# Low parts of the weights formed by TensorE, the softmax epsilon added by GpSimd, and a new order, in a windowed attention with a gated feed-forward

## The chip, the cores and the metric

One core of one Trainium2 chip runs the kernel. The metric is the device time of one execution in microseconds (us); a time "before" is the median of three runs.

## What is computed

Eight batches of eight heads, 576 positions, 64 numbers per head. Each position attends to itself and the 63 positions before it. The attention's output x (576 by 512 per batch) then goes two ways: through a causal depthwise convolution of 5 taps and a sigmoid (the gate), and through a 512 by 512 matrix (the value). Their product goes through a second 512 by 512 matrix.

```python
scores = np.where(mask, scores, -1000000000.0)
scores = scores - np.max(scores, axis=-1, keepdims=True)
attn = np.exp(scores)
attn = attn / (np.sum(attn, axis=-1, keepdims=True) + 1e-09)
x = np.matmul(attn, v)                       # then heads side by side
for k in range(K):
    gate_pre += conv_w[k][None, None, :] * xp[:, k:k + S, :]
gate = 1.0 / (1.0 + np.exp(-gate_pre))
val = x @ w_val
return (gate * val @ w_out).astype(np.float32)
```

The weights arrive as 64-bit floats, and the kernel takes their words apart itself.

## The kernel before

The attention is worked off in 16 windows w (two per batch). A window has two parts g of 5 and 4 column tiles, for each of which the kernel runs, with hh the half of the heads:

- `S(w,g)`: TensorE (PE) forms the scores, 80 or 64 small matmuls (L522), into PSUM slots `s`;
- `M(w,g),hh`: VectorE (DVE) adds the mask and takes the minimum (L543);
- `X(w,g),hh`: ScalarE (ACT) takes the exponentials and accumulates the sums of the rows (L553);
- `R(w,g)`: DVE adds 1e-9 to the sums and takes the reciprocal. The sums stand in a tile with two numbers per row, the second set to 1e-9 once; L561 reduces over the two, L562 is the reciprocal;
- `N(w,g),hh`: DVE, ACT or GpSimd (POOL) scales by it (L572, L574); `T(w,g),hh`: DVE transposes in 32x32 blocks (L580);
- `AVw_n`: PE multiplies with v, in steps of 16 matmuls (L611).

`EX` copies the result out of PSUM, `XH` rounds it to the short format float32r, and `XL` (POOL, L762) is the rest, so that a product of two numbers becomes three float32r matmuls. The convolution is `C` on DVE and ACT (L811, L814), or for two heads' pairs `K` on PE in plain float32 (L779); `SIG` is the sigmoid of a batch's gate. `V` is one block of the value matrix, 12 matmuls of 288 columns (L855); `HF` (DVE, L866) multiplies it with the gate; `HH` and `HL` split the product; `O` is one block of the output matrix, 12 matmuls of 512 columns (L921); `EO` copies it out and `DO` stores it. `LQ`, `LV` and `LW` are loads.

The weights come in eight pieces of 128 by 512, `w0` to `w3` of the value matrix and `w4` to `w7` of the output matrix (function `split_f64`). A piece takes DVE, ACT and POOL steps `h`, `k`, `b`, `c`, `p`, `u`, `l` on the words; `H` (ACT, L449) rounds the high part; `l` (L440, or L470 after `u`) gives the contribution of the low word; and the low part is then (a - high) + l, in two steps, `r` (L452, subtract) and `s` (L455, add). Of these 16 steps 12 are on POOL and four on DVE.

Nothing is scheduled by the framework: the table `ORDER` lists all steps, with the engine behind a slash, and each engine gets its instructions in that order. Each engine then runs its own list in order and waits on semaphores. PSUM has two slots `f` that `V`, `O`, `K` and fillers share. A word like `*2+11` in the table puts filler matmuls in front of the next step: here 2 big ones (512 columns, plain float32, L1034) and 11 small ones (512 columns, float32r, L1036), whose results nobody reads. Before has 10 big and 13 small fillers.

Of the kernel before, what the change touches and what calls it, by code (L numbers as in the profile page):

```python
# [8 lines left out]
F32 = mybir.dt.float32  # L9
# [18 lines left out]
    flex=dict(EO='AV', HH='AG', XH='AG', HL='G', CC='A', N='GAV', EX='AV', WR='GV', WK='GV', WL='GV', XL='G', DG='GV', C0='A', WH='VA'),  # L28
# [7 lines left out]
    half=(),  # L36
# [26 lines left out]
C2_3 S(3,1) XH3/A XL2 C3_3 X((3,0),0) K0_0 LQ10_0 C2_2 LV3 LQ11_0 CC0_1 X((3,0),1) w1r/G XL3 C3_2 M((3,1),0)
M((3,1),1) S(4,0) C2_1 w5s/G V0_0_2_0 C3_1 w1s/G C2_0 CC0_0 X((3,1),0) w6h/A C3_0 FX0 N((2,1),0)/G w7h/A R(3,0)
AV2_0 AV2_1 w6k/V V0_1_1_0 w7k/V w6b SIG0_0 T((2,1),0) N((3,0),1)/G T((2,1),1) w7b AV2_2 w6c AV2_3 AV2_4 AV2_5 w7c
AV2_6 AV2_7 AV2_8 HF0_0_2 w7p V0_0_0_0 w6p HF0_1_1 HH0_0_2_0/G M((4,0),0) HH0_1_1_0/G AV2_9 M((4,0),1) w7u AV2_10
V0_1_0_0 HL0_0_2_0 N((3,0),0)/G w6u X((3,1),1) T((3,0),1) EX4/A HL0_1_1_0 C4_4 HF0_0_0 T((3,0),0) w6l/G R(3,1)
EX5/A V0_0_1_0 C4_3 w7H HH0_0_0_0/G w7l/G HF0_1_0 C5_4 C4_2 S(4,1) N((3,1),1)/A HH0_1_0_0/A X((4,0),0) C5_3 w7r/G
V0_0_3_0 HF0_0_1 LQ12_0 M((4,1),0) N((3,1),0)/A LQ13_0 LV4 C4_1 C5_2 HH0_0_1_0/G HL0_0_0_0 w7s/G HF0_0_3 C5_1
V0_1_2_0 V0_1_3_0 HL0_0_1_0 M((4,1),1) X((4,1),0) w6H HH0_0_3_0/G C5_0 HL0_0_3_0 S(5,0) C4_0 X((4,0),1) w6r/G  # L70
T((3,1),1) T((3,1),0) AV3_0 AV3_1 AV3_2 w6s/G HF0_1_2 AV3_3 X((4,1),1) AV3_4 M((5,0),1) HF0_1_3 AV3_5 AV3_6 CB0 FX1
AV3_7 R(4,0) AV3_8 N((4,0),1)/V AV3_9 AV3_10 O128_0_0 HH0_1_2_0/A M((5,0),0) XH4/A HL0_1_0_0 HH0_1_3_0/A R(4,1)
EX6/A C6_4 EX7/A HL0_1_3_0 C6_3 T((4,0),1) S(5,1) EO128_0/A C7_4 C6_2 N((4,0),0)/G HL0_1_2_0 O256_0_0 XH5/G XH6/G
LQ14_0 X((5,0),0) M((5,1),0) T((4,0),0) C6_1 XL6 XH7/G DO128_0 N((4,1),1)/G XL4 C7_3 X((5,0),1) C7_2 O384_0_0 XL5
R(5,0) M((5,1),1) C7_1 EO256_0/A X((5,1),0) XL7 FX3 FX2 S(6,0) EO384_0/V X((5,1),1) DO256_0 T((4,1),1) C7_0 LV5
LQ15_0 O0_0_0 N((4,1),0)/G C6_0 N((5,0),1)/G M((6,0),0) T((4,1),0) SIG1_0 AV4_0 EO0_0/V M((6,0),1) AV4_1 AV4_2
AV4_3 AV4_4 AV4_5 AV4_6 AV4_7 AV4_8 R(5,1) T((5,0),1) AV4_9 AV4_10 V1_1_0_0 EX8/A N((5,1),0)/V N((5,0),0)/V DO0_0
LV6 C8_4 XH8/G EX9/A V1_0_2_0 C8_3 C9_4 XL8 XH9/G HF1_1_0 C8_2 V1_0_1_0 X((6,0),0) HF1_0_2 C9_3 HH1_0_2_0/A S(6,1)
XL9 HF1_0_1 T((5,0),0) V1_1_1_0 DO384_0 LQ16_0 HH1_0_2_1/A HH1_1_0_0/A X((6,0),1) FX4 M((6,1),0) T((5,1),0) LQ17_0
C8_1 HL1_0_2_0 HH1_0_1_0/G N((5,1),1)/G HL1_1_0_0 V1_0_3_0 HF1_1_1 X((6,1),0) R(6,0) HH1_1_1_0/G HH1_0_1_1/G  # L80
M((6,1),1) T((5,1),1) C9_2 HL1_1_1_0 V1_0_0_0 N((6,0),0)/A HL1_0_1_0 HL1_0_2_1 S(7,0) HF1_0_3 HF1_0_0 HH1_0_0_0/A
HH1_0_0_1/G X((6,1),1) N((6,0),1)/A C9_1 C8_0 HH1_0_3_0/G HL1_0_0_0 V1_1_3_0 HL1_0_1_1 HL1_0_0_1 M((7,0),1)
HL1_0_3_0 V1_1_2_0 HH1_0_3_1/G HF1_1_3 C9_0 HL1_0_3_1 R(6,1) HH1_1_3_0/A AV5_0 AV5_1 HF1_1_2 AV5_2 HL1_1_3_0 AV5_3
CB1 HH1_1_2_0/A AV5_4 N((6,1),0)/A AV5_5 AV5_6 HL1_1_2_0 AV5_7 T((6,0),0) AV5_8 AV5_9 AV5_10 N((6,1),1)/G
T((6,1),0) M((7,0),0) O896_0_0 EX10/A LV7 C10_4 XH10/G EX11/A C10_3 C11_4 XH11/G T((6,0),1) XL11 XL10 C10_2
O768_0_0 EO896_0/A C11_3 X((7,0),0) C10_1 C11_2 FX5 V2_0_0_0 C11_1 C10_0 C11_0 X((7,0),1) EO768_0/A S(7,1) DO768_0
# [24 lines left out]
M((12,1),1) T((11,0),0) LQ29_0 C18_4 HL3_1_1_0 HL3_1_3_0 M((12,1),0) HL3_1_2_0 O2048_0_0 C18_3 EO1792_0/A
# [974 lines left out]
```

## Time and profile before

| | us |
|---|---|
| median of three runs | 330.45 (328.34 to 330.98) |
| the profiled execution | 327.39 |
| its span, first to last instruction | 325.6 |
| PE busy | 311.8 |
| DVE busy | 250.3 |
| ACT busy | 245.7 |
| POOL busy | 179.5 |

The span is 1.8 us shorter than the execution's own time. Every step below is measured in the profiled execution.

### The profile page before, as it was taken

What the parts mean: (1) busy time and instruction counts of PE and PEld (TensorE: products, weight loads), DVE (VectorE), ACT (ScalarE), POOL (GpSimd) and SP (SyncE); (2) the same over time, 40 slices, a digit from 0 to 9 for tenths busy, and PEclk for the clock granted to TensorE, in tenths of its full rate; (3) what the DMA queues carried; (4) which work ended last, traced back from release to release, by engine and by line L of the source; (5) the groups of instructions that cost most, each with busy time, mean ns of one, the idle gap of its engine ahead of it and who ended that gap; (6) DMA issues with size and microseconds to landing.
All of it is one profiled execution on the core that took longest, in us unless ns stands there. A gap on an engine that the chain in (4) does not pass through costs nothing.

```text
span 325.6 us, 15010 instructions
## 1 busy us (share of the span) xinstructions
PE 311.8 (96%) x6149; PEld 263.0 (81%) x6149; DVE 250.3 (77%) x973; ACT 245.7 (75%) x835; POOL 179.5 (55%) x247
## 2 busy tenths in 40 slices
PE   7699989999999999999999899999999999999996
PEld 3355658887799877898889778898889889989985
DVE  4999989999999896999788587989786956272200
ACT  3798998999899898987899688996788663334111
POOL 4245386699858831775646815458147731761710
PEclk9799999999999999999999999999999999999999
DMA  7997765263466246652617282710243311002012
GB/s 252 321 314 197 251 190 170 71 202 88 149 203 205 69 142 194 205 181 76 195 37 229 73 251 88 206 68 31 90 137 89 142 68 48 4 32 97 2 64 97
DMA packets 28227, 45.02 MB, mean 138 GB/s; under 512 B 3968, under 2 KB 15488, under 8 KB 28160
## 3 DMA queue, kind: packets, MB, share of 16 engines
q1 hardware_dynamic: 27728, 43.60, 42.7%
q8 instruction: 48, 0.79, 1.0%
q10 hardware_dynamic: 432, 0.48, 0.5%
q14 instruction: 19, 0.16, 0.1%
HBM read 34.62 MB, written 9.44 MB: 135 GB/s over the span
## 4 chain that ended last, share of the span: by engine, by line
PE 81%; DVE 11%; ACT 4%; issue 2%; DMA 1%; ACTq 0%; DVEq 0%
PE f L921 32%; PE f L855 29%; PE av L611 10%; PE s L522 8%; DVE p L543 3%; DVE gp L811 3%; ACT p L553 2%; DMA st<-in_w_val_dram 1%; PE f L1034 1%; PE f L1036 1%; DVE pts L580 1%; DVE hf L866 1%; DVE w0l L440 0%; ACT xh L239 0%; ACT x L239 0%
## 5 line engine op out<-in xcount | busy, mean ns | idle before, releaser
L553 ACT ACTIVATE p<-p,nm 128x96 f32<-128x96 f32 x288 | 103.9, 364 | 4.7 <-DVE nm L543 4.5
L811 DVE SCALAR_TENSOR_TENSOR gp<-av,cw,gp 128x575 f32<-128x575 f32 (+3 forms) x120 | 93.4, 801 | 6.8 <-ACT gp L814 5.9
L855 PE MATMUL f<-xl,wv_hi 128*128 128x288 f32 x256 | 77.9, 304 | 0.6 <-DVE hf L866 0.5
L855 PE MATMUL f<-xh,wv_hi 128*128 128x288 f32 x256 | 75.5, 295 | 0.7 <-issue 0.7
L855 PE MATMUL f<-xh,wv_lo 128*128 128x288 f32 x256 | 75.4, 294 | 0.0
L884 POOL TENSOR_TENSOR h_lo<-hf,h_hi 128x288 fp32r<-128x288 f32 (+2 forms) x80 | 54.3, 693 | 19.8 <-ACT h_hi L239 19.2
L543 DVE CUSTOM_DVE_ANT_0 p<-s,mask 128x96 f32<-128x96 f32 x288 | 54.6, 250 | 6.8 <-PE s L522 6.4
L921 PE MATMUL f<-wo_hi,h_lo 128*128 128x512 f32 (+1 forms) x148 | 59.3, 400 | 0.0
L762 POOL TENSOR_TENSOR xl<-x,xh 128x576 fp32r<-128x576 f32 x32 | 45.6, 1435 | 24.0 <-ACT xh L239 23.5
L921 PE MATMUL f<-wo_lo,h_hi 128*128 128x512 f32 (+1 forms) x148 | 57.8, 390 | 1.0 <-issue 1.0
L921 PE MATMUL f<-wo_hi,h_hi 128*128 128x512 f32 (+1 forms) x148 | 57.7, 390 | 0.0
L553 ACT ACTIVATION_READ_ACCUMULATOR p<-p,nm 128x1 f32 x288 | 54.3, 189 | 0.0
L855 PEld LDWEIGHTS f<-xl,wv_hi 128*128 128x128 f32 x256 | 48.0, 188 | 3.6 <-DVE hf L866 1.0
L866 DVE TENSOR_TENSOR hf<-f,gp 128x288 f32<-128x288 f32 x64 | 28.5, 450 | 28.3 <-PE f L855 20.7
L855 PEld LDWEIGHTS f<-xh,wv_lo 128*128 128x128 f32 x256 | 48.1, 188 | 0.9 <-issue 0.8
L855 PEld LDWEIGHTS f<-xh,wv_hi 128*128 128x128 f32 x256 | 48.1, 188 | 0.5
L574 POOL TENSOR_TENSOR p<-p,rc 128x384 f32<-128x384 f32 (+1 forms) x38 | 35.0, 927 | 23.6 <-DVE rc L562 19.9
L522 PE MATMUL s<-ktb,qtb 64*32 64x96 f32 x2304 | 37.2, 248 | 5.5 <-DVE nm L543 3.2
L611 PEld LDWEIGHTS av<-pts,v 32*64 32x64 f32 x2560 | 35.1, 130 | 8.3 <-issue 5.3
L580 DVE STREAM_TRANSPOSE pts<-p 128x480 f32<-128x480 f32 (+1 forms) x64 | 38.2, 610 | 4.1 <-PE av L611 3.0
L522 PEld LDWEIGHTS s<-ktb,qtb 64*32 64x32 f32 x2304 | 29.5, 105 | 13.8 <-issue 12.7
L611 PE MATMUL av<-pts,v 32*64 32x96 f32 (+2 forms) x2560 | 39.2, 244 | 0.1
(129 smaller groups left out, 411.1 us busy)
## 6 DMA issues: line engine op xcount, KB each, us to landing
out_dram<-ot SPq DMA_DIRECT2D x35, 256.0 KB, 3.1
qtb<-in_qT_dram SPq DMA_DIRECT2D x30, 288.0 KB, 3.8
ktb<-in_kT_dram SPq DMA_DIRECT2D x30, 288.0 KB, 4.0
v<-in_vw_dram SPq DMA_DIRECT2D x64, 96.0 KB, 3.2
v<-in_vw_dram SPq DMA_DIRECT2D x64, 80.0 KB, 3.1
st<-in_w_val_dram SPq DMA_DIRECT2D x4, 512.0 KB
st<-in_w_out_dram SPq DMA_DIRECT2D x2, 1024.0 KB, 6.5
out_dram<-ot SPq DMA_DIRECT2D x2, 128.0 KB
```

The costliest lines, as they stand in the source:

```text
L522: nc.tensor.matmul(sp_t[m, hh][z * Q:z * Q + Q, t, :], lhsT=held("qt", i)[r, c:c + Q], rhs=held("kt", i)[r, c:c + KW], start=True, stop=True)
L543: nc.vector.tensor_tensor_reduce(out=pe[:, t, :], in0=sp_t[u][:, t, :], in1=mask_of(w, n0 + t), scale=-SCALE, scalar=3.0e38, op0=ALU.add, ...
L553: nc.scalar.activation(out=pe[:, t, :], in_=pe[:, t, :], func=AF.Exp, scale=-1.0, bias=nm[:, t:t + 1], accum_out=su[:, t:t + 1])
L574: MUL[e](out=pe, in0=pe, in1=rc.unsqueeze(2).broadcast_to([P, ng, KW]))
L580: nc.vector.transpose(out=pts_t[w, hh][:, n0 * KW:n1 * KW], in_=p_t.pop(u).rearrange("p t k -> p (t k)"))
L611: nc.tensor.matmul(av_t[w, z // 2][hh * D:(hh + 1) * D, c + lo * Q:c + hi * Q], lhsT=v_t[w][z * Q:z * Q + Q, hh, m % 2, m // 2 - KEYS[th][ ...
L762: SUB[e](out=batch_tile(xl_t, "xl", b, F32R)[:, hp, :], in0=x_t[i // 2][:, i % 2, :], in1=xh_t[b][:, hp, :].bitcast(F32))
L811: nc.vector.scalar_tensor_tensor(out=acc, in0=av(i, 0, S - back), scalar=col, in1=acc, op0=ALU.mult, op1=ALU.add)
L855: nc.tensor.matmul(vp_t[u][:, 0:NH], lhsT=w[:, c, js], rhs=x[:, c, hs], start=(a + z == 0), stop=(a + z == NM - 1))
L866: nc.vector.tensor_mul(out=hf, in0=free_f[-1][:, 0:NH], in1=gp_t[b][:, jb, hs])
L884: SUB[e](out=h_lo[:, jb, dst:dst + hi - lo], in0=hf_t[u][:, lo:hi], in1=h_hi[:, jb, dst:dst + hi - lo].bitcast(F32))
L921: nc.tensor.matmul(op_t[key][:, 0:cs.stop - cs.start], lhsT=h[:, jb, col:col + P], rhs=w[:, jb, cs], start=(a + z == 0), stop=(a + z == NM ...
```

## The change

The low part of every weight piece is formed on PE: three matmuls into a slot `f` add identity times a (plain float32), minus identity times the high part, and identity times `l` (both float32r). This is the step `e`; the step `s` is now a copy of the result out of PSUM, on ACT (five) or DVE (three). Steps `r` are gone. Two more constant matrices, `plus` and `minus`, are made on ACT. The tile of the sums has one number per row; a new step `Z` adds 1e-9 to it, on POOL (22 times) or DVE (10), and `R` is the reciprocal alone. The table `ORDER` is written anew, with 7 big and 42 small fillers, and was planned with the loads of instruction pieces placed by where PE's sequencer stands; the code that did that is not part of the kernel. The buffers of the convolution's diagonal matrices are named otherwise, with the same two in use.

```diff
-    sums = [const.tile([P, 2, PARTS[1], 2], F32, name=f"sums{n}") for n in range(4)]
-    for t in sums:
-        nc.vector.memset(t, 1.0e-9)
+    sums = [const.tile([P, 2, PARTS[1]], F32, name=f"sums{n}") for n in range(4)]
     ident = const.tile([P, P], F32, name="ident")
     make_identity(nc, ident)
+    plus = const.tile([P, P], F32R, name="plus")
+    minus = const.tile([P, P], F32R, name="minus")
+    nc.scalar.copy(out=plus, in_=ident)
+    nc.scalar.activation(out=minus, in_=ident, func=AF.Copy, scale=-1.0)
...
+    ON_PE = ('w0', 'w1', 'w2', 'w3', 'w4', 'w5', 'w6', 'w7')
...
+        if on_pe:
+            def rest(_):
+                g = low_t[name] = free_f.pop(0)
+                nc.tensor.matmul(like(g), lhsT=ident, rhs=like(t["af"]), start=True, stop=False)
+                nc.tensor.matmul(like(g), lhsT=minus, rhs=hi, start=False, stop=False)
+                nc.tensor.matmul(like(g), lhsT=plus, rhs=like(t["lr"]), start=False, stop=True)
+
+            def out(e):
+                free_f.append(low_t.pop(name))
+                COPY[e](out=lo, in_=like(free_f[-1]))
+            r1 = op(name + "e", ("P", 1319), rest, [hi_, lw], take=[("ps_f", name)], prio=prio)
+            return [hi_, op(name + "s", pick("EO", A=95 + 427 * c, V=70 + 535 * c), out, [r1],
+                            free=[(tag, name), ("ps_f", name)], prio=prio)]
...
+        def e_z(e):
+            BOTH[e].tensor_scalar(out=sums_of(m), in0=sums_of(m), scalar1=1.0e-9, scalar2=None, op0=ALU.add)
+        z2 = op(f"Z{m}", pick("Z", G=100, V=150), e_z, xs, prio=prio, port="VG")
+
         def e_r(_):
             rc = rc_t[m] = sb("rc", [P, 2, ng], f"rc{w}_{g}", bufs=4)
-            nc.vector.tensor_reduce(out=rc, in_=sums_of(m), axis=mybir.AxisListType.X, op=ALU.add)
-            nc.vector.reciprocal(out=rc, in_=rc)
-        r2 = op(f"R{m}", ("V", 318), e_r, xs, prio=prio)
+            nc.vector.reciprocal(out=rc, in_=sums_of(m))
+        r2 = op(f"R{m}", ("V", 165), e_r, [z2], prio=prio)
```

Of the table, the start, before and after:

```diff
-LC LW1_0 LQ0_0 LQ1_0 LQ0_1 LW0_0 w2h/A LQ1_1 cwh/V cwk/V w2k/V w2b cwb w2b LW1_1 cwc w2c LQ2_0 w2p w2H w2l/V cwH *3+1
...
+LC LW1_0 LQ0_0 LQ1_0 LW1_1 LQ1_1 LQ0_1 LQ2_0 LW0_0 LQ3_0 cwh/V w2h/V w2k/V w2b cwk/G w2c w2p w2l/V w2H w3h/A w3k/G
+*2+11 S(0,0) cwb M((0,0),0) M((0,0),1) *0+4 w2e *0+2 S(0,1) w2s/V cwc w3b cwp w3c w3p M((0,1),0) M((0,1),1) w3l/V
```

The first place is PE's list between the first two score blocks. In the kernel before, the last matmuls of S(0,0) (tiles s_0_0 and s_0_1) are followed at once by those of S(0,1) (s_1_0 and s_1_1):

```order
L522 MATMUL s_0_0_178<-ktb_84,qtb_80 32x96
L522 MATMUL s_0_1_179<-ktb_84,qtb_80 32x96
L522 MATMUL s_1_0_260<-ktb_83,qtb_79 32x96
L522 MATMUL s_1_1_261<-ktb_83,qtb_79 32x96
L522 MATMUL s_1_0_260<-ktb_83,qtb_79 32x96
```

In the changed kernel the same place holds fillers (L1064) and the three matmuls of piece w2's low part (L488 to L490, into f):

```order
L544 MATMUL s_0_0_191<-ktb_84,qtb_80 32x96
L544 MATMUL s_0_1_192<-ktb_84,qtb_80 32x96
L1064 MATMUL f_64<-h_lo 128x512 x4
L488 MATMUL f_64<-w2a,ident 128x512
L489 MATMUL f_64<-wv_hi,minus 128x512
L490 MATMUL f_64<-w2l,plus 128x512
L1064 MATMUL f_65<-h_lo 128x512 x2
L544 MATMUL s_1_0_257<-ktb_83,qtb_79 32x96
L544 MATMUL s_1_1_258<-ktb_83,qtb_79 32x96
```

Six fillers and a low part now stand ahead of S(0,1) on PE; five more low parts stand in the same way before the first V block, and two (w7, w6) between V blocks of the first batch.

The second place is the start of ACT's list, before:

```order
L951 DMA cwords<-in_conv_w_dram 128x40
L336 DMA qtb_80<-in_qT_dram 128x448
L337 DMA ktb_84<-in_kT_dram 128x448
L414 ACT_TABLE_LOAD
L414 ACTIVATE w2m<-st_141 128x512
```

and in the changed kernel:

```order
L979 DMA cwords<-in_conv_w_dram 128x40
L341 DMA qtb_80<-in_qT_dram 128x448
L260 ACT_TABLE_LOAD
L260 CAST plus<-ident 128x128
L261 ACTIVATE minus<-ident 128x128
L342 DMA ktb_84<-in_kT_dram 128x448
L458 CAST wv_hi<-w2a 128x4x128
```

The load of a k tile that S(0,0) needs now stands behind the table load and the two new constants on ACT.

## Rows read from the trace of the kernel before

**Rows 1.** The page: busy us (share of the span) by engine.
```profile
PE 311.8 (96%) x6149; PEld 263.0 (81%) x6149; DVE 250.3 (77%) x973; ACT 245.7 (75%) x835; POOL 179.5 (55%) x247
```

**Rows 2.** The ending chain in order of time: start us, us, what.
```profile
69.13 0.38 DVE hf L866
...
69.55 1.85 PE f L855 x12
...
72.59 2.43 PE av L611 x119
...
322.64 0.37 ACT ot L239
```

**Rows 3.** PE by stretches: from:to, length, PE busy (instructions), clock, DMA, GB/s.
```profile
0.00:12.90 12.90, 8.14 (x152) 1.00 0.87 304
12.90:16.40 3.50, 3.50 (x5) 0.51 0.96 214
16.40:72.50 56.10, 52.00 (x1295) 1.00 0.65 201
72.50:322.60 250.10, 248.12 (x4704) 1.00 0.37 115
```

**Rows 4.** The same chain: one block or several of AV, S, V, O.
```profile
97.09 4.97 PE f L855 x36
102.06 1.13 PE s L522 x68
...
116.14 0.93 PE s L522 x56
117.07 2.19 PE av L611 x112
...
252.98 8.43 PE f L921 x36
...
269.41 9.57 PE f L855 x72
```

**Rows 5.** PE's timeline: first fillers, S(0,0), fillers at 12.8 us, one K block.
```profile
1.45 5.15 PE L1034 MATMUL f<-ident 128*128 128x512 f32 x6 [1.45 <-POOL ident masks.py:199]
...
7.52 1.25 PE L522 MATMUL s<-ktb,qtb 64*32 64x96 f32 x80 [0.68 <-DMA ktb<-in_kT_dram]
...
12.79 3.65 PE L1034 MATMUL f<-ident 128*128 128x512 f32 x4
15.45 1.49 PE L1036 MATMUL f<-h_lo 128*128 128x512 f32 x2
...
36.10 2.69 PE L779 MATMUL f<-x,dg 128*128 128x288 f32 x10
```

**Rows 6.** The same chain: fillers between steps of AV0.
```profile
23.40 1.06 PE f L1034 x2
24.45 0.23 PE f L1036
```

**Rows 7.** ACT's timeline at the start (ACTq: its DMA issues).
```profile
1.74 0.45 ACTq L337 DMA_DIRECT2D ktb<-in_kT_dram  x1
2.22 1.28 ACT L414 ACT_TABLE_LOAD   x1 [2.22 <-issue]
```

**Rows 8.** Groups by line: busy us, mean ns, idle before.
```profile
L561 DVE TENSOR_REDUCE rc<-sums 128x10 f32<-128x20 f32 x16 | 2.6, 163 | 1.2 <-ACT p L553 1.1
L455 DVE TENSOR_TENSOR wv_lo<-w0m,w0l 128x512 fp32r<-128x512 f32 x1 | 0.7, 679 | 0.0
L452 POOL TENSOR_TENSOR w0m<-w0a,wv_hi 128x512 f32<-128x512 f32 x1 | 1.3, 1278 | 0.0
L455 POOL TENSOR_TENSOR cl<-cwm,cwl 128x20 fp32r<-128x20 f32 x1 | 0.2, 223 | 0.0
```

**Rows 9.** PE's timeline: the two longest waits after 72.5 us.
```profile
122.28 0.50 PE L921 MATMUL f<-wo_lo,h_hi 128*128 128x512 f32 x1 [0.96 <-issue]
180.26 0.29 PE L855 MATMUL f<-xh,wv_hi 128*128 128x288 f32 x1 [0.74 <-issue]
```

More of the change, by code (lines that the diff above doesn't have):

```diff
@@ L150 @@
+EO4352_0/A O4480_1_0 DO4352_0 CB7 FX15 EO4480_1/A DO4480_1 CB6 FX14
 """.split()
@@ L400, in tile_window_attention_gated_ffn @@
     lows = []
+    ON_PE = ('w0', 'w1', 'w2', 'w3', 'w4', 'w5', 'w6', 'w7')
+    low_t = {}
     def split_f64(name, words, rows, n, hi, lo, tag, load, prio, free=()):
+        on_pe = name in ON_PE
         t = {}
@@ L412, in head @@
                 t[x + "f"] = t[x].bitcast(F32)
+            t["lr"] = t["l"].bitcast(F32R) if on_pe else t["lf"]
             if e == "A":
@@ L439, in low @@
             if e == "V":
-                stt(out=t["lf"], in0=u, scalar=2.0 ** -52, in1=t["mf"], op0=ALU.mult, op1=ALU.mult)
+                stt(out=t["lr"], in0=u, scalar=2.0 ** -52, in1=t["mf"], op0=ALU.mult, op1=ALU.mult)
             else:
-                nc.gpsimd.tensor_scalar(out=t["lf"], in0=u, scalar1=2.0 ** -52, scalar2=None, op0=ALU.mult)
-                nc.gpsimd.tensor_mul(out=t["lf"], in0=t["lf"], in1=t["mf"])
+                nc.gpsimd.tensor_scalar(out=t["lr"], in0=u, scalar1=2.0 ** -52, scalar2=None, op0=ALU.mult)
+                nc.gpsimd.tensor_mul(out=t["lr"], in0=t["lf"], in1=t["mf"])
         def like(x):
@@ L465, in number @@
             def number(_):
-                nc.scalar.activation(out=t["lf"], in_=t["low"].bitcast(mybir.dt.uint32), func=AF.Copy, scale=2.0 ** -52)
+                nc.scalar.activation(out=t["lr"], in_=t["low"].bitcast(mybir.dt.uint32), func=AF.Copy, scale=2.0 ** -52)
             lw = [pw, op(name + "u", ("A", 110 + 470 * c), number, [a], prio=prio)]
             def low(e):
-                MUL[e](out=t["lf"], in0=t["lf"], in1=t["mf"])
+                MUL[e](out=t["lr"], in0=t["lf"], in1=t["mf"])
             at = pick("WR", G=130 + 1065 * c, V=70 + 535 * c)
@@ L549, in e_x @@
             def e_x(_, u=u, hh=hh):
[L550 removed]
+                su = sums_of(m)[:, hh, :]
                 pe, nm = p_t[u], nm_t.pop(u)
@@ L696, in e_cv @@
                     lo = back if y == 0 else 0
-                    nc.tensor.matmul(g[:, lo:NH], lhsT=dg[:, (KP.index(hp) * TAPS + kk) * P:(KP.index(hp) * TAPS + kk + 1) * P],
+                    nc.tensor.matmul(g[:, lo:NH], lhsT=dg[:, (hp % 2 * TAPS + kk) * P:(hp % 2 * TAPS + kk + 1) * P],
                                      rhs=x(t0 + lo - back, t0 + NH - back), start=back == 0, stop=kk == 0)
@@ L778, in e_cv @@
                         lo = back if half == 0 else 0
-                        nc.tensor.matmul(g[:, lo:NH], lhsT=dg[:, (KP.index(hp) * TAPS + kk) * P:(KP.index(hp) * TAPS + kk + 1) * P],
+                        nc.tensor.matmul(g[:, lo:NH], lhsT=dg[:, (hp % 2 * TAPS + kk) * P:(hp % 2 * TAPS + kk + 1) * P],
                                          rhs=x_t[i // 2][:, i % 2, half * NH + lo - back:half * NH + NH - back],
@@ L782, in attention @@
                 cv = op(f"K{i}_{half}", ("P", 500 * (TAPS - end)), e_cv, [ex, dgo[hp], xl_o if half else None], take=[("ps_f", (i, half))], words=4 * (TAPS - end) + 1,
-                        prio=cp)
+                        free=[(f"dg{hp % 2}", hp)] if half else [], prio=cp)
+                if half:
+                    cv.deps.append(last_cv)
+                last_cv = cv
                 def e_cc(e, half=half):
@@ L969, in tile_window_attention_gated_ffn @@
     KP = sorted({i % NHP for i, c in enumerate(CFG["conv"]) if c == "K"})
-    dg = const.tile([P, max(len(KP), 1) * TAPS * P], F32, name="dg")
+    dg = const.tile([P, 2 * TAPS * P], F32, name="dg")
     dgo = []
@@ L978, in e_dg @@
             t = slice(hp * TAPS, (hp + 1) * TAPS)
-            MUL[e](out=dg.rearrange("p (t n) -> p t n", n=P)[:, KP.index(hp) * TAPS:(KP.index(hp) + 1) * TAPS, :], in0=ident.unsqueeze(1).broadcast_to([P, TAPS, P]),
+            MUL[e](out=dg.rearrange("p (t n) -> p t n", n=P)[:, hp % 2 * TAPS:(hp % 2 + 1) * TAPS, :], in0=ident.unsqueeze(1).broadcast_to([P, TAPS, P]),
                    in1=cw[:, t].unsqueeze(2).broadcast_to([P, TAPS, P]))
-        dgo.append(op(f"DG{hp}", pick("DG", V=740, G=1450), e_dg, [cwo], prio=CFG["dg"][hp], port="VG"))
+        dgo.append(op(f"DG{hp}", pick("DG", V=740, G=1450), e_dg, [cwo], take=[(f"dg{hp % 2}", hp)], prio=CFG["dg"][hp], port="VG"))
     w_ops = [[], []]
```

203 lines of the change are left out of this document (101 added, 102 removed).

## The prediction

> **What bounds the kernel now.** I read the page first, then the chain that ended last in order of time, then PE's busy time by stretches. On the page PE is busy for 96% of the span, DVE for 77%, ACT for 75% [rows 1]; 96% is a mean, so the next question is where the rest lies. The chain in order of time says where: up to 69.55 us it keeps going through DVE (the last such piece is an hf), and from there to 322.64 it is PE alone, until the last copy out [rows 2]. So the kernel has two halves with different rules. From 72.59 on (PE begins AV3, the products of window 3) the end is "when AV3 starts, plus the PE work behind it". In that stretch PE idles 250.10 - 248.12 = 1.98 us. Ahead of it PE idles 4.76 + 4.10 = 8.86 us, and for 3.5 us it ran at half its clock (0.51: the 1.2 GHz level) [rows 3]. What other engines save counts only ahead of AV3, and only as far as PE is not itself late there.
>
> I therefore make the sum in two terms: the time at which PE reaches AV3, and what is lost behind it.
>
> **PE's work behind AV3** is the same in both tables: 21 S blocks, 13 AV, 56 V, 37 O (two of half width), no low part; one small filler is new (0.23 [rows 6]). Changes from a block of small matmuls (S, AV) to V, O or a filler cost about 0.18 each: 36 V matmuls behind an S take 4.97, by the rate of 72 of them (9.57/72 = 0.133 each) 4.79 [rows 4]. There are 30 such changes behind AV3 in either table. So this part differs by 0.2 us, plus waits.
>
> **PE's work ahead of AV3.** Block times at full clock: S 1.13 or 0.93, AV 2.19, V 12 x 0.133 = 1.60, O matmul 8.43/36 = 0.234 [rows 4], K 2.69 less its overlap of some 0.02, 2.67 [rows 5]. A big filler: the first three took 5.15, 1.72 each; two more with two small ones, nearly all at the half clock, took 15.45 + 1.49 - 12.79 = 4.15 [rows 5]; so 1.72 is a price at the low level and 0.86 one at the high level. Alone behind an AV step it took 1.06 [rows 6], which is 0.86 and the change of 0.2. A small filler is 0.23 there; I take 0.215 in a run of them. A low part has no row. It has one plain float32 matmul of 512 columns, like a big filler, and two float32r ones, like two O matmuls: 0.86 + 0.47 = 1.33. Its bounds are 1.42, by K's 2.67/5 = 0.53 for 288 columns scaled to 512 (0.95), and 1.53 by the lone filler above; below, 0.70, three O matmuls. I take 1.33, since the big filler has the same shape and type.
>
> After, ahead of AV3: 11 S (6 x 1.13 + 5 x 0.93 = 11.4), AV0 to AV2 (6.6), 4 K (10.7), 8 V (12.8), 8 low parts (10.6), 7 big fillers (6.0), 41 small ones (8.8), 13 changes from small matmuls at 0.2 (2.6), the start at 1.45, and the low level at first: 2 big ones at 1.72 and some 3 small ones at twice their time (2.4). Sum 73.3.
>
> Before, by the same prices: S, AV, K, V as above (41.5), 10 big (8.6), 13 small (2.8), 18 changes (3.6), the start 1.45, three big ones at the low level (2.6), and half of the 3.4 us at half clock (1.7): 62.3. With the 8.86 us of idle time that is 71.1; the trace has 72.6. The sum is 1.5 short, by small steps between fillers and AV steps, of which there are fewer after.
>
> So after, **PE is full from the start to AV3 even if it never waits**, and reaches it at 73.3 where before it was at 72.6 with 8.9 us of waiting. Low parts and fillers fill the gaps, and a little more. Next, one wait that the change adds. ACT now issues the load of a k tile behind its table load (1.28) and two small casts (some 0.3 each, worked out from the 0.2 of small operations [rows 8]), so at some 3.6 instead of 1.74 [rows 7]. S(0,0) waited for just this kind of load before, 0.68 until 7.52 [rows 5]. The fillers ahead of it end at 1.45 + 3.4 + 3 x 0.43 + 8 x 0.215 = 7.9. With the load 1.9 later S(0,0) would start at up to 9.4, and if the queue of transfers is the limit rather than the issue, at 7.9. I take 8.8, 0.9 of waiting; behind S(0,0) stand all of PE's fillers and low parts, so it passes on to AV3 whole. AV3 at 74.2: **+1.6 us**, between 0 (the low part at 0.70, the load hidden: 73.3 - 5.0 would be less than DVE allows, below) and +6 (gaps stay, below).
>
> **What the other engines save.** DVE loses 32 reduces of about 0.16 (5.0) and four adds or subtracts of 0.68; it gains three copies of about 0.7 and ten additions of some 0.16 to 0.2, and takes over a few copies and scalings from ACT. POOL loses 12 steps of 1.28 (15.4) and gains 22 small additions of about 0.22, the size of its 128x20 operation [rows 8]. Ahead of the first sigmoid, which the V blocks wait for through hf, this makes DVE's list shorter by seven reduces (1.1) and two full operations (1.4), less three additions (0.5): about 2 us. Before, DVE was the pace there, so DVE alone would allow AV3 at 70.6. PE doesn't: its sum is 73.3. That is why I cost the whole relief at nothing: the cover that hides it is PE's new work, and if that were gone, it would be worth those 2 us. Z adds a hop X to POOL to DVE to the chain of each part; behind AV3 its cover is that DVE and ACT have 250 and 246 us of work for 325 [rows 1].
>
> **Waits behind AV3.** Of the 1.98 us, 0.96 and 0.74 stand as "issue": in mid block, with nothing to wait for [rows 9]. The first comes two us behind S and AV back to back, 56 and 112 recorded matmuls in 3.1 us, each with its weight load [rows 4], the second by the table behind S(12,0) and the first steps of AV9; that looks like instructions that arrive late. The new table has seven such neighbours of S and AV behind AV3, the old six, so the risk is still there, and the table was planned to keep clear of it. Between all gone (-2.0) and one more of the larger size (+1.0) I take -0.5.
>
> The Trainium skill, "Runtime: NRT & Kernel Launch", section "Instruction fetch mechanics", says that instructions stream in by blocks of 256 and that this is hidden, because the sequencer issues more slowly than the blocks arrive. This case's trace speaks against it where small matmuls stand thick: 0.96 and 0.74 us without another cause [rows 9]. If the rule held, the two waits would be something else, the new table could do nothing about them, and this term would be 0, not -0.5.
>
> **Sum.** +1.6 + 0.2 - 0.5 = +1.3 on the profiled execution's 327.39: 328.7. The median of the runs shown is 330.45, 0.9% above the profiled one; for the time to be measured I put the same 1.3 us on the median: 331.7, rounded to 331.5.
>
> **The rivals.** About 1% (3.3 us) is what a measurement of this kernel can tell from no change; faster and slower mean by more than that.
>
> First rival, slower: low parts wait in PE's queue. Each waits for its high part from ACT and its product l from DVE or POOL, and everything behind it on PE waits too: the next S, hence M, X and all that follow. For it speaks that PE's list is full, so that a gap can't be made up; before, gaps of 8.86 us stood in the same stretch [rows 3]. Against it: between S blocks PE has slack against DVE (DVE's list is as long as PE's there), and fillers stand where waits were planned. If half of the old gaps stay, AV3 comes 4.4 later: 331.7 + 4.4 = 336. It decides from gaps of 2.0 us on (1.3 + 2.0 = 3.3). Chance 0.25, with a half-clock spell of 3.5 us at the start, as before, as a smaller form of it (1.7).
>
> Second rival, faster: PE's work ahead of AV3 is overpriced, DVE stays the pace and gives its 2 us, and the waits behind AV3 go: -2.0 - 2.0 = -4.0, 326.5. For it: DVE in the chain up to 69.5 [rows 2]. Against it: the low part would have to cost 1.33 - 2.7/8 = 1.0 or less, under what its float32 matmul and two O matmuls took; and there is no more than 1.98 us to gain behind AV3. Chance 0.10.
>
> Third rival, the table's care for instruction pieces does nothing, or the seven dense spots stall more: then 332 to 333, inside my own case.
>
> **How the numbers follow.** My case, within 1% of before, has 0.65; slower 0.25; faster 0.10. The range goes from 328.0 (the waits gone, the low part cheap: -2.5) to 336.0 (half the gaps stay), which leaves out some 0.1 on each side.
>
> **What would show it right or wrong.** Right: PE's first AV3 matmul at 73 to 76 us; PE idle ahead of it under 3 us in place of 8.9; a low part with 1.3 to 1.5 us; 250 us from AV3 to the last matmul. Wrong: AV3 before 72 us (then DVE set the pace and PE was overpriced), AV3 after 77 us with waits in front of low parts or of S(0,0), a half-clock spell after 8 us, or more than 3 us of "issue" behind AV3. POOL's additions would be wrong at nothing if R or N are seen waiting for them with PE idle behind.

## The result and the profile after

The changed kernel took 332.56 us (median of 20 runs, 329.72 to 334.48), the kernel before, beside it on the same chip, 330.49 (20 runs, 326.12 to 334.59). Between the medians that is 2.07 us, 0.63%; the ratio is 1.0104, with an interval of 1.0074 to 1.0134. Ratios and intervals, here and below, leave out the executions that lie more than 1.5% above the fastest of the same kernel (of the kernel before 7 of the 20), while medians are those of all. So it is slower by about 1%, at the edge of what can be told from no change, and inside the range of the prediction, 1.1 us above its number. The profiled executions lie further apart: 327.39 before (span 325.6) and 331.37 after (span 329.6). The 4.0 us between them are what can be followed in rows; the medians say that about half of that is typical.

The page after, for [rows 1], with one row of its queues (packets, MB, share):

```profile
PE 321.3 (97%) x6204; PEld 272.0 (83%) x6204; DVE 252.6 (77%) x949; ACT 237.8 (72%) x818; POOL 183.8 (56%) x272
...
q8 instruction: 49, 0.80, 1.0%
```

PE has 9.5 us more to do. The second row is used further down: 49 pieces of instructions, 0.80 MB, so 16 KB each. PE by stretches, for [rows 3] (from:to, length, PE busy with its instructions, clock, DMA share, GB/s), cut at the start of AV3 and once more where the half-clock spell lay before:

```profile
0.00:12.90 12.90, 11.47 (x169) 1.00 0.89 296
12.90:16.40 3.50, 3.50 (x23) 1.00 0.78 256
16.40:78.00 61.60, 58.84 (x1332) 1.00 0.64 188
78.00:326.60 248.60, 247.46 (x4702) 1.00 0.36 114
```

Two things changed places. Ahead of AV3 PE does 11.47 + 3.50 + 58.84 = 73.81 us of work where it did 63.64, its idle time falls from 8.86 to 1.43 + 2.76 = 4.19, the half-clock spell is gone, and AV3 comes at 78.0 instead of 72.6: 5.4 later. Behind it the last copy out begins 248.6 us later instead of 250.1: 1.5 less, and PE idles 1.14 instead of 1.98. 5.4 - 1.5 = 3.9, but for rounding the 4.0 between the profiles.

The ending chain in order of time, for [rows 2, 4, 6] (start us, us, what):

```profile
8.07 1.12 PE s L544 x69
...
10.32 0.86 PE f L488 x2
11.18 0.23 PE f L489
11.41 0.23 PE f L490
...
28.83 1.46 PE s L544 x68
...
51.00 7.06 DMA ktb<-in_kT_dram
58.06 0.14 issue
58.20 1.12 PE s L544 x63
...
64.33 8.14 PE f L883 x60
72.47 0.86 PE f L488 x2
...
78.02 2.19 PE av L636 x116
...
326.63 0.37 ACT ot L242
```

A low part takes 0.86 + 0.23 + 0.23 = 1.32, as priced (the trace has four matmuls for it, since the plain float32 one shows as two). Up to 58 us the chain passes through loads, the last of them that of a k tile, and no longer through DVE: the load that S(4,0) needs began to be issued at 51.00. PE's waits say what that cost (engine, line, what for: us in total, times, longest):

```profile
PE s L544 <- DMA ktb<-in_kT_dram: 1.7, 1, 1.7
PE f L1062 <- POOL ident masks.py:199: 1.4, 1, 1.4
PE f L1064 <- POOL h_lo L912: 1.0, 1, 1.0
PE av L636 <- DMA v<-in_vw_dram: 0.6, 1, 0.6
PE av L636 <- DVE pts L605: 0.3, 1, 0.3
```

There is no "issue" among them, which is time in which the engine waited for nothing that the profile shows; before, PE had three such waits, 3.1 us together, two of them in [rows 9]. The 1.0 is new: a small filler behind S(12,0) at 178.8 us, which reads h_lo and stands until POOL has written it. The 1.7 is S(4,0); SP's timeline shows why its load is late:

```profile
37.30 12.52 SPq L362 DMA_DIRECT2D v<-in_vw_dram  x16
49.86 0.58 SPq L393 DMA_DIRECT2D st<-in_w_out_dram  x1
...
51.00 0.44 SPq L342 DMA_DIRECT2D ktb<-in_kT_dram  x1
```

LV2 and LV3 are 16 transfers, 0.78 us apart on average in SP's queue, and LW3 and LQ9 stand behind them. S(4,0) is begun at 56.11, and waits until 58.20.

### The profile page after: what moved, and what is told of

It reads as the page before. It is cut to its first block, busy times and chain, and to the rows that moved or that the text cites. A ratio compares the mean times of both kernels' runs of the same rounds, so it can differ in the third digit from the quotient of the medians.

```text
span 329.6 us, 15091 instructions
## 1 busy us (share of the span) xinstructions
PE 321.3 (97%) x6204; PEld 272.0 (83%) x6204; DVE 252.6 (77%) x949; ACT 237.8 (72%) x818; POOL 183.8 (56%) x272
## 4 chain that ended last, share of the span: by engine, by line
PE 88%; DMA 6%; SPq 2%; POOL 2%; DVE 1%; issue 1%; ACT 0%; ACTq 0%; POOLq 0%
PE f L949 31%; PE f L883 31%; PE av L636 11%; PE s L544 9%; DMA st<-in_w_out_dram 3%; PE f L1064 2%; DMA ktb<-in_kT_dram 2%; PE f L804 2%; SPq L362 2%; PE f L488 1%; PE f L1062 1%; DMA v<-in_vw_dram 1%; POOL h_lo L912 1%; DVE p L565 0%; POOL h_hi L249 0%
## 5 line engine op out<-in xcount | busy, mean ns | idle before, releaser
L599 POOL TENSOR_TENSOR p<-p,rc 128x480 f32<-128x480 f32 (+1 forms) x38 | 34.7, 921 | 15.6 <-DVE rc L587 15.1
L636 PE MATMUL av<-pts,v 32*64 32x96 f32 (+2 forms) x2560 | 38.3, 244 | 1.0 <-DMA v<-in_vw_dram 0.6
```

Source lines behind the costliest of these rows:

```text
L599: MUL[e](out=pe, in0=pe, in1=rc.unsqueeze(2).broadcast_to([P, ng, KW]))
L636: nc.tensor.matmul(av_t[w, z // 2][hh * D:(hh + 1) * D, c + lo * Q:c + hi * Q], lhsT=v_t[w][z * Q:z * Q + Q, hh, m % 2, m // 2 - KEYS[th][ ...
```

## The experiments

Two theories on the 5.4 us at AV3. **P:** PE's own list sets AV3, so what is taken off PE ahead of it comes off its start. **Q:** a chain of loads, ACT and DVE sets it, and PE only fills up. And one question on the table: are the "issue" waits a matter of where instructions stand, and what would they cost. The kernel before ran beside each group; its medians were 329.63 (e1 to e4), 330.40 (e5 to e8) and 330.17 (e9 to e12). An AV3 time is that of its first matmul. From a single profile it is good to about 1 or 2 us: AV2, ahead of which the changed kernel, e1 and e9 have the same lists, begins at 59.25, 57.65 and 56.92, and executions of the changed kernel alone have spans from 327.9 to 332.7.

**e1: the low parts of w6 and w7 back on POOL.** They are the two between V blocks just ahead of AV3, 2.64 us of PE.

```diff
-    ON_PE = ('w0', 'w1', 'w2', 'w3', 'w4', 'w5', 'w6', 'w7')
+    ON_PE = ('w0', 'w1', 'w2', 'w3', 'w4', 'w5')
-... w7e ... w7s/A ... w6e ... w6s/V
+... w7r/G ... w7s/G ... w6r/G ... w6s/G
```

> The changed kernel, but the low parts of w6 and w7 alone are formed by POOL in two steps, as in the kernel before. My theory (PE is full from about 59 us on, so what it is spared there comes off the end): PE's list loses 2 x 1.32 us; AV3 starts 2.6 us earlier than 78.0, the time falls by 2 to 3 us (0.6 to 0.9%). Rival (the low parts lie in gaps that other engines leave): no change beyond 0.5 us, or slower, because POOL has 5 us more to do while it also splits the products of the first batch.

334.47 us, 1.0164 (1.0107 to 1.0222). AV3 began at 73.70, 4.2 us earlier than in the changed kernel. Its 160 matmuls in PE's timeline (start us, us, what, and in brackets the idle time before with what ended it):

```profile
73.70 0.38 PE L636 MATMUL av<-pts,v 32*64 32x96 f32 x8
74.38 0.81 PE L636 MATMUL av<-pts,v 32*64 32x96 f32 x40 [0.29 <-DVE gp L839]
76.34 1.21 PE L636 MATMUL av<-pts,v 32*64 32x96 f32 x72 [1.16 <-DVE pts L605]
77.96 1.29 PE L636 MATMUL av<-pts,v 32*64 32x64 f32 x40 [0.42 <-issue]
```

Of the 4.2, AV2 had 1.6 already. From the first matmul of AV2 to that of AV3 PE took 16.05 us instead of 18.70, shorter by 2.65 where 2.64 were taken off: up to there PE's list is full, and P holds. But AV3 itself then stood, mostly for DVE, and its last matmul came at 78.96 instead of 79.99, so counted from AV2 0.6 later. What PE was spared had become waits. From 77.60 to 84.60 PE then ran at half its clock:

```profile
77.60:84.60 7.00, 6.64 (x114) 0.51 0.27 73
84.60:329.00 244.40, 242.34 (x4469) 1.00 0.36 114
```

7.0 us at the 1.2 GHz level do the work of 3.5, so the gaps in AV3 cost more than their length in this execution. They are not the whole loss: two of the six executions had a mean clock of 1.000, with spans of 330.3 and 333.9. e4 and e9, with the same edit, came out alike (below): all three are 0.6% over the changed kernel's 1.0104, so by the times these two low parts are better on PE, as the rival had it.

**e2: the k tile of S(4,0) ahead of the v tiles in SP's queue.**

```diff
-CC0_0 K0_1 LQ8_0 LV2 LV3 LW3 LQ9_0 X((3,0),1)
+CC0_0 K0_1 LQ8_0 LQ9_0 LV2 LV3 LW3 X((3,0),1)
```

> The changed kernel with one load moved: the q and k tiles LQ9, which S(4,0) needs, go ahead of the v loads LV2 and LV3 and of the w_out words LW3 in SP's list. My theory (16 v transfers occupied SP's queue from 37.3 to 49.9 us, so LQ9 was issued at 50.5 and S(4,0) stood at 56.1 until 58.2): the wait of 2.1 us in S(4,0) goes, AV3 starts at about 76, the time falls by 1.5 to 2 us, if v arrives in time for AV2. Rival (PE would next wait for something else there, the hf of the first V block behind the sigmoid): the wait moves to V0_0_1 or AV2 and the time falls by less than 0.7 us.

332.92 us, 1.0110 (1.0058 to 1.0163). In PE's waits the one for the k tile shrank, and a longer one took its place:

```profile
PE av L636 <- DVE gp L839: 2.7, 1, 2.7
...
PE s L544 <- DMA ktb<-in_kT_dram: 0.7, 1, 0.7
```

LW3, now last in SP's queue, had its words in late (issued at 50.59, 6.32 us), DVE's step on w6 waited for them, and so did what stands behind it on DVE, which AV waited for. AV3 came at 79.05. That is the rival's outcome: the wait moved to AV2. Of the loads near 50 us, the one that went last was waited for in both orders.

**e3: no filler behind S(12,0).**

```diff
-HL3_0_0_1 *0+1 V3_0_3_0
+HL3_0_0_1 V3_0_3_0
```

> The changed kernel without the one small filler that stands behind S(12,0). It reads h_lo, which POOL writes just then, and PE idled 1.0 us in front of it at 177.8. My theory: the wait and the filler go (1.0 + 0.2 to 0.5), the time falls by 1.0 to 1.5 us. Rival (the V block behind it would wait for the same: its slot f is freed by hf): PE idles there all the same and nothing changes.

332.27 us, 1.0039 (0.9984 to 1.0093). The 1.0 us wait for h_lo is gone and nothing came in its place there: from the first matmul of S(12,0) to that of the next V block PE took 1.13 us instead of 2.58. A gain in the whole time is not shown. By the medians this run lies 0.8% above the kernel before, the changed kernel 0.63%; from AV3 to the last copy out its profile has 248.4 us, the changed kernel's 248.6; and e10, with the same edit, came out at 1.0069.

**e4: e1, e2 and e3 together.**

> The three edits of e1 to e3 together. My theory (each takes its time off the same full engine, one after the other): they add up, -5 to -6 us against the changed kernel, 1% faster than the kernel before or a little less. Rival (what PE is spared is lost again to DVE's pace ahead of AV3): no more than -3 us.

335.64 us, 1.0171 (1.0109 to 1.0232), the rival's outcome. AV3 began at 75.18, and its last matmul came at 79.74. The three waits are gone or shorter, and others stand there: 1.6 for pts, 1.5 for gp, and 0.8 for wo_lo, which POOL now makes late.

**e5: ACT's and DVE's first steps on w4 moved behind work that is ready.** Ahead of AV0 ACT stood 2.5 us for w4's words, whose transfer took 8.87.

```diff
-w0c w4h/A X((1,0),0) X((1,0),1) w0H w4u
+w0c X((1,0),0) X((1,0),1) w0H w4h/A w4u
...
-w0p w4k/V N((0,1),1)/V
+w0p N((0,1),1)/V
...
-w0l/V Z(1,0)/G
+w0l/V w4k/V Z(1,0)/G
```

> The changed kernel with ACT's first step on piece w4 (w4h, which waits for the words of w_out) behind the exponentials X(1,0) and w0H, and DVE's w4k behind w0l. In the changed kernel ACT stood 2.5 us in front of w4h until the words had landed at 22.7 us. New theory Q (the start is paced by a chain through loads, ACT and DVE, and PE's new work lies mostly in its gaps): that wait goes, AV3 starts 1 to 2.5 us earlier than 78.0, the time falls by 1 to 2 us. My first theory P (PE's own list ahead of AV3 is full and sets AV3's start): no change of AV3's start beyond 0.5 us.

332.28 us, 1.0066 (1.0035 to 1.0098), AV3 at 77.61, 0.4 earlier: no more than P expected, and not the 1 to 2.5 of Q. The waits ahead of AV3 were now 1.1 for ACT's gp in front of low parts and 0.7 of "issue": another exchange.

**e6: the new table with no low part on PE.** All eight go to DVE and POOL, on the engines of the kernel before.

```diff
-    ON_PE = ('w0', 'w1', 'w2', 'w3', 'w4', 'w5', 'w6', 'w7')
+    ON_PE = ()
```

> The new table, but no low part on PE: every e and s is again a subtraction and an addition on the engines of the kernel before (12 on POOL, 4 on DVE), at the places where e and s stood; fillers as in the changed kernel. Theory P: PE's list loses 8 x 1.32 = 10.6 us ahead of AV3, so AV3 starts some 4 us earlier (until the next limit) and the time falls by 3 to 4 us. Theory Q: PE only idles more (its idle time ahead of AV3 rises from 4.2 to about 13 us), AV3's start stays within 1.5 us of 78.0 or comes later, for POOL and DVE get 18 us back, and the time is the same or up to 2 us longer.

351.34 us, 1.0650 (1.0586 to 1.0714), which neither theory had. AV3 began at 85.60, 7.6 later, and its last matmul came at 90.15; ahead of it PE idled 14.0 us, about as Q had it. PE's waits:

```profile
PE av L636 <- issue: 5.9, 6, 1.7
PE av L636 <- DVE pts L605: 4.2, 2, 2.6
PE s L544 <- DVE nm L565: 3.9, 3, 2.7
```

POOL was busy for 201.1 us instead of 183.8, and with ACT it makes up the chain from 62 to 95 us. In this table the low parts on PE are thus worth far more than their price. And the "issue" waits came back, with 32 matmuls fewer ahead of the same S and AV blocks.

**e7: the new table without fillers.**

```diff
-... *2+11 S(0,0) ... *0+4 w2e *0+2 S(0,1) ...
+... S(0,0) ... w2e S(0,1) ...
```

> The changed kernel without any filler matmul (7 big, 42 small, together 16 us of PE with those at the low clock level). Theory P: PE reaches AV3 earlier by what fillers pushed back, 3 to 6 us, less what half-clock spells cost (1.7 us for each 3.4 us). Theory Q: AV3's start moves by less than 1.5 us; PE's idle time ahead of it rises by over 8 us, and the granted clock shows at least one half spell more, so the time is the same or 1 to 3 us longer.

356.26 us, 1.0766 (1.0684 to 1.0848), far longer than either theory had it; of Q the idle time and the half-clock spells came true. AV3 came at 84.7, with 17.5 us of idle time ahead of it, and the stretch behind it, whose only edit is one filler, took 17.8 us longer. PE by stretches:

```profile
0.00:84.60 84.60, 67.09 (x1448) 0.86 0.62 193
84.60:351.00 266.40, 253.28 (x4701) 0.98 0.33 106
...
104.00:105.40 1.40, 1.40 (x97) 1.00 0.92 281
105.40:109.00 3.60, 0.03 (x1) 0.77 0.24 91
109.00:114.20 5.20, 5.19 (x51) 0.50 0.23 64
```

(The last three rows are another cut, around one wait.) Of the 17.8, 13.12 - 1.14 = 12.0 are idle time and 253.28 - 247.46 = 5.8 work at half clock. "issue" is the largest of its waits, 19.3 us in 12 places over the whole span:

```profile
PE av L636 <- issue: 12.0, 7, 3.6
PE s L544 <- DMA ktb<-in_kT_dram: 7.9, 3, 7.4
PE s L544 <- issue: 6.0, 4, 2.2
...
PE f L949 <- issue: 1.3, 1, 1.3
```

The longest, in the middle of an AV step, from 105.43 to 109.01:

```profile
109.01 1.30 PE L636 MATMUL av<-pts,v 32*64 32x96 f32 x42 [3.58 <-issue]
```

The transfers by queue, of 106.5 to 107.0 us (queue: packets, MB, share), and the stretch ahead of them, in the form of the stretches:

```profile
q8 instruction: 1, 0.02, 11.7%
...
105.40:106.30 0.90, 0.03 (x1) 1.00 0.85 328
```

PE had been dry for over 1.0 us when this piece began to move, and went on 2.0 to 2.5 us after that, at half clock. Along the whole spans of five kernels (before, after, e6, e7, e12) PE has 33 "issue" waits of 0.25 us or more (3, 0, 6, 12, 12). In all 33 a piece began to move 1.7 to 3.6 us before the wait ended, counted from the start of its half microsecond, nearly always 2.4 to 3.2. A kernel has 48 or 49 pieces in some 330 us, one in 7 us, so that is no chance meeting: "issue" here is the wait for instructions.

The single records of the five traces settle it. Count PE's matmuls, weight loads and semaphore instructions from 0: in 32 of the 33 waits the first instruction that was late has the same place in a run of 256, number 193. So a piece holds 256 instructions, and these waits stand where one piece ends. All 32 ended 1.3 to 1.6 us after the last byte of the piece had landed, and at the boundaries without a wait PE never went on sooner than 1.25 us after it. (The 33rd, 2.23 us at 15.24 in e7, has neither mark and is something else.) In the median a piece began to move 1.1 us after PE had begun on the one ahead of it, and moved for about 1 us; with the 1.4 behind the landing that makes some 3.5 us. A run of 256 that PE works off faster mostly ends in a wait: of the 21 runs that held PE for less than 2.2 us, 18 did, and of the 182 of over 4 us, 5. Those 21 are S and AV blocks and little else. In the changed kernel the shortest run holds PE for 3.39 us, and there is no wait.

Where PE needed longer for the 256 and waited all the same, the piece had mostly started late, and there the transfer engines were mostly full. In the 2 us ahead of the 32 pieces their busy share is 0.58 on average, ahead of the others 0.41, but in 7 of the 32 it is under 0.1. Other transfers seem to add to these waits, then, and are not needed for one.

**e8: the sums as before, without Z.**

```diff
-    sums = [const.tile([P, 2, PARTS[1]], F32, name=f"sums{n}") for n in range(4)]
+    sums = [const.tile([P, 2, PARTS[1], 2], F32, name=f"sums{n}") for n in range(4)]
+    for t in sums:
+        nc.vector.memset(t, 1.0e-9)
...
-            nc.vector.reciprocal(out=rc, in_=sums_of(m))
+            nc.vector.tensor_reduce(out=rc, in_=sums_of(m), axis=mybir.AxisListType.X, op=ALU.add)
+            nc.vector.reciprocal(out=rc, in_=rc)
```

> The changed kernel with the sums as before: two numbers a row, DVE reduces and takes the reciprocal, no step Z on POOL or DVE. Prediction on record (the relief of DVE is worth nothing): within 0.7 us. Rival 1 (DVE paces the start, its 5 us less count): 1 to 2 us longer than the changed kernel. Rival 2 (the hop over POOL costs, since DVE waited 1.2 us for Z and POOL's additions stood 7.4 us for ACT's sums): 0.5 to 1.5 us shorter.

332.53 us, 1.0088 (1.0045 to 1.0131), AV3 at 77.7: the same, as predicted. Z is worth nothing either way, though DVE waits for it (3.4 us in two places in the changed kernel).

**e9: e1 with six small fillers where each of the two low parts stood.**

```diff
-... w7r/G S(5,0) ... w6r/G AV3_0
+... w7r/G *0+6 S(5,0) ... w6r/G *0+6 AV3_0
```

> The run e1 (low parts of w6 and w7 on POOL) with six small fillers (1.3 us) on PE at each of the two places where these low parts stood. In e1 PE waited 1.2 us for DVE's pts ahead of AV3, its granted clock then stood at the half level from 77.7 to 84.5 us, and AV3 came no earlier. Theory Q (DVE and POOL set AV3's start, and PE's low parts also keep its clock up): with fillers the half-clock spell is gone and the time falls by 1 to 3 us against e1, to that of the changed kernel within 1 us. Rival (POOL's added work is what e1 lost): no change against e1, 334 to 335 us.

334.28 us, 1.0166 (1.0113 to 1.0218). AV3 came at 75.76, and its last matmul at 77.81, 2.2 us earlier than in the changed kernel; all of it is there at AV2 already (56.92 for 59.25), and the twelve fillers make the way from AV2 to AV3 as long as the low parts did (18.84 us for 18.70). But POOL, with the two pieces back, is late with wo_lo (PE's timeline, then PE by stretches):

```profile
82.10 0.50 PE L949 MATMUL f<-wo_lo,h_hi 128*128 128x512 f32 x1 [1.78 <-POOL wo_lo L464]
```

```profile
75.70:83.20 7.50, 5.72 (x235) 1.00 0.27 70
83.20:86.70 3.50, 3.50 (x10) 0.51 0.43 139
```

1.8 of waiting and 1.7 of half clock take the gain back, so the time is that of e1, as the rival had it. In this execution, then, what the low parts of w6 and w7 on PE buy is not AV3 but wo_lo in time for the first O block; e4 waits for wo_lo too (0.8), e1 does not.

**e10: e3 and e5 together. e11: e10, with the loads of k tiles and weight words ahead of v tiles in two places.**

```diff
-LV1 LW0_1 S(2,0)
+LW0_1 LV1 S(2,0)
...
-LQ8_0 LV2 LV3 LW3 LQ9_0
+LQ8_0 LQ9_0 LW3 LV2 LV3
```

> The changed kernel with the edits of e3 (the late filler gone) and e5 (w4h later). If each keeps its gain (e3 0.6%, e5 0.4% by their medians against the changed kernel's 1.0104), they add up to about 1.0000 of the kernel before; if both gains were the spread between executions, 1.005 to 1.010.

> e10 with SP's list mended at two places: LQ9 and the words LW3 both ahead of the v loads LV2 and LV3 (16 transfers, 12.5 us of SP's queue), and the words LW0_1 ahead of LV1. In e2 LQ9 alone went ahead, LW3 fell behind, and DVE then waited for its words (w6) until 57.5 us, so that PE waited 2.7 us for DVE ahead of AV2. Theory Q (the start is paced by loads through DVE): neither wait is left, AV2 starts 1.5 to 2.5 us earlier than 59.3, the time falls by 1.5 us or more against e10. Rival P (PE's own list): less than 0.7 us, as in e2.

e10: 332.14 us, 1.0069 (1.0025 to 1.0113), AV3 at 78.85: by what was put on record, the gains of e3 and e5 were the spread between executions. e11: 333.77 us, 1.0126 (1.0056 to 1.0196), though its profiled execution has the shortest span of all changed versions, 328.6. In it AV2 begins at 56.23, 3.0 earlier than in the changed kernel, but AV3 only 0.8 earlier, at 77.25. In both the "issue" waits are back (1.5 and 2.4 us). No version beat the kernel before.

**e12: the low parts of w0 to w5 on PE in the table of before.** Sums, w6 and w7 as before; each `r` becomes an `e`, and four `s` go to ACT or DVE.

```diff
-S(0,0) w2r/V ... w2s/G
+S(0,0) w2e ... w2s/V
```

> One part alone: the kernel before, its table and fillers, with the low parts of w0 to w5 on PE at the places of the subtractions; copies out on DVE (w0, w2, w3, w4) and ACT (w1, w5), in places moved up where the slots f ask for it; w6, w7 and the sums as before. PE gets 6 x 1.32 = 7.9 us more ahead of AV3, where it idled 8.9; POOL loses 10 us, DVE about nothing. Theory Q (it lies in gaps): within 1.5 us of the kernel before. Theory P (PE's list ahead of AV3 sets its start): 3 to 6 us longer.

362.01 us, 1.0896 (1.0814 to 1.0978), far outside both theories. PE's waits and PE by stretches, cut at its AV3:

```profile
PE av L632 <- issue: 16.2, 9, 3.3
PE s L543 <- issue: 2.6, 3, 1.6
```

```profile
0.00:80.90 80.90, 72.31 (x1473) 0.98 0.63 196
80.90:356.00 275.10, 259.83 (x4707) 0.96 0.34 105
```

AV3 came 8.4 us later, 4.0 of it in two "issue" waits. Behind AV3 this kernel has the table of before, word for word, and took 275.1 us for it instead of 250.1: 13.3 more idle, and 11.7 more work, at half clock. What differs is what went ahead: 24 more matmuls, each with its weight load, have gone through PE's sequencer, and every piece of instructions ends elsewhere. The same half of the idea that costs 1% in its own table costs 9% in another.

## Why the prediction was right, and where it was not

**The sum.** +1.3 was forecast on the profiled execution; it was +4.0 there and +2.1 between the medians. By the ratio the likeliest case, within 1%, is missed by 0.04%, by the medians it is met; the number was missed by 1.1 us. The mechanism held: the end is "when AV3 starts, plus the work behind it", PE became nearly full ahead of AV3, and what the other engines were spared brought nothing. Two sizes were off, of opposite sign, so that the number came so near is in part luck: AV3 was 3.8 us later than forecast, 1.2 of that came back behind it, and the medians lie only half as far apart as the profiles. By the prediction's own signs, the low part and the time behind AV3 came out right, AV3's start (78.0 for 73 to 76) and PE's idle time ahead of it (4.19 for under 3) did not.

**The start of AV3: 74.2 forecast, 78.0 seen.** Half of the 3.8 is PE's own list: 73.3 was the sum with the 1.45 at the start, 73.81 + 1.43 = 75.2 was seen. The same shortfall could be read in the kernel before: there the sum counts the 1.45 twice, since it is part of the 8.86 of idle time, so the check gives 69.7 for 72.6 and is 2.9 short, not 1.5. The low part was right (1.32 for 1.33). S and AV blocks among low parts were too cheap: S(2,0) has 1.46 in the chain for 1.13, and AV0 and AV1, taken in pieces, 2.57 and 2.47 for 2.19, 1.0 together; S(4,0), broken in two by its wait, adds 0.4 (0.43 + 1.12 for 1.13). The rest I can't name. The other half is waits: 2.76 for the 0.9 I had. The 0.9 itself, S(0,0) behind the later load from ACT, did not occur: S(0,0) followed the fillers at 8.07 without a gap. In its place came S(4,0)'s k tile (1.7), v for AV0 (0.6) and pts (0.3), the first two from the new order of the loads, which I had read for its first lines only. "DVE alone would allow AV3 at 70.6" failed too, as a step: DVE's stretch ahead of AV3 reads

```profile
0.00:78.00 78.00, 67.95 (x295) 1.00 0.69 209
```

and the same stretch of before (0 to 72.5 us) has 65.57 us of work, so its list there had not become shorter by 2; nor does it set AV3's start now, with 10 us idle.

**Was PE the bound then?** From AV2 to the first matmul of AV3, yes: taking 2.64 us off PE shortened that way by 2.65 (e1), and twelve fillers in the same places made it as long as in the changed kernel (e9). But not alone. The rest of AV3 then waited for DVE, and was over no sooner, counted from AV2; ahead of AV2, moving one late load made the next one late (e2), and the first steps on w4 likewise (e5). PE's list, the loads and the chain through ACT and DVE end within a microsecond or two of each other; each edit only chose which is seen. That is also the first rival's picture, gaps that stay in PE's queue, in its small form: 2.76 us of gaps, not in front of low parts but of S and AV.

**Behind AV3: +0.2 - 0.5 forecast, -1.5 seen.** The two "issue" waits went altogether (-1.7), and the small filler, priced at its 0.23, waited 1.0 for h_lo (e3). In sum 0.8 of the gain is less idle time, and 0.7 is work, 247.46 for 248.12. I had taken the table's care for instruction pieces for a term of half a microsecond, and as the third rival for one that could do nothing; the time came out at that rival's 332 to 333, but not by its mechanism. This was the largest error of judgement, though not of number. e6, e7 and e12 have 5.9, 19.3 and 19.2 us of "issue" waits, where the changed kernel has none. The Trainium skill, "Runtime: NRT & Kernel Launch", section "Instruction fetch mechanics", says that the fetch is hidden since the sequencer issues more slowly than blocks arrive. These runs disagree in places where S and AV stand thick: 32 waits at piece boundaries of up to 3.58 us in five kernels. With that rule e7 would have lost its fillers' time and the loads' wait, and not 17.8 us behind AV3.

**The relief of the other engines at nothing, Z at nothing.** Right, by e8 for Z. For the rest there was hardly any relief to cost: by the page DVE has 252.6 us for 250.3 and POOL 183.8 for 179.5, and only ACT has less, 237.8 for 245.7, since the new table moved steps from ACT to both (DVE copies x out 10 times for 6, POOL rounds xh 20 times for 14). The prediction had named such steps for DVE and given them no price, and none for POOL. And it holds only with the low parts where they are: with these steps and the twelve on POOL (201.1 us), this table loses 19 us (e6).

**What stays open.** The share of each of the three causes in the 5.4 us, since each cure brought another wait; why the medians of e10 and e11 do not follow their profiles; and whether a boundary moved on purpose, and nothing else, takes such a wait away, since no run here did that alone. The clock doesn't explain the spread: the 20 executions of the changed kernel had a mean granted clock of 0.994 to 1.000 and spans from 327.9 to 332.7, and at 1.000 alone just as wide a spread. Nor does it explain the loss: of 17 executions of the kernel before beside e1, 16 were below 1.000, down to 0.979, and they were faster all the same. Whether a table with e9's start and a POOL that is in time with wo_lo would beat the kernel before was not tried.

## What to carry to other kernels

Where small matmuls stand back to back, the position of every instruction on PE is a resource of its own: adding or taking away a few instructions far ahead moves where the next piece of instructions is wanted, and can cost more than the work that was added. After any such edit, count the "issue" waits in PE's list before arguing about anything else, and count PE's instructions in runs of 256: the runs to look for are those that small matmuls fill alone, which PE works off in 2 us. And before moving work onto the engine that waits, look at what it waits for: where several chains end together, filling one engine's gaps only changes the name of the wait, and the start of a step says little when the step can wait within itself (AV3 in e1). A filler that reads a tile still being written is itself a wait.

## What the runs showed of the hardware

- PE's instructions come in pieces of 256, and 32 waits stand where one ends; each was over 1.3 to 1.6 us after the next had landed.
- A wait for instructions in mid block took up to 3.58 us (e7). In that one the engine had been dry for over 1.0 us when the 16 KB piece moved, and resumed some 2 us after. That half microsecond has only five other packets, but the transfer engines were busy at 0.85 from 105.4 to 106.3 us, just ahead of it, so other transfers may have held the piece up; that is not shown.
- Gaps on PE were often followed by a spell at half clock: 3.58 us in e7 (clock 0.50 in the stretch behind it), 1.78 in e9, 1.16 and 0.42 in e1, 1.9 in e3 (half clock from 59.08, for 3.41 us). Not each one: behind the 1.66 of the changed kernel at 58.2 the clock stayed at 1.00. A spell of 3.5 us does the work of half its length, so a gap of under 2 us can cost nearly twice itself.
- Sixteen transfers of v issued by SP in one go hold its queue for 12.52 us, and what stands behind them is late by as much, though each is small (80 or 96 KB).
